# Modulation rows by TensorE alone, with unused products in its queue

## The chip, the cores and the metric

The kernel runs on one core of one Trainium2 chip. The metric is the device time of one execution in microseconds (us), as the median of several runs. Besides these, one execution was recorded by the hardware profiler; all views of the profile and of the trace are of that one.

The engines of the core are called as the profile calls them: PE is TensorE, the matrix engine (PEld is its loading of weights), DVE is VectorE, ACT is ScalarE, POOL is GpSimd, and SP is the queue from which most transfers are issued. Each works through its own instructions in the order in which they were written, and they meet through semaphores.

## The reference, cut to what matters

One sequence of 2048 tokens with 1024 channels goes through two modulated blocks: a Fourier mixing of tokens and channels, and an MLP with 3584 hidden units. Six rows of 1024 values that depend only on the vector `c` modulate them. Everything is float32.

```
mod = (_silu(c) @ w_mod).reshape(c.shape[0], 6, 1, -1)        # c: 1 x 1024, w_mod: 1024 x 6144
sa, ca, ga, sb, cb, gb = (mod[:, 0], mod[:, 1], ..., mod[:, 5])
h = _layernorm(x, axis=-1) * (1 + ca) + sa
x = x + ga * _A_ref(h, dft_seq_re, dft_seq_im, dft_hid_re, dft_hid_im)
h = _layernorm(x, axis=-1) * (1 + cb) + sb
x = x + gb * _B_ref(h, w1, b1, w2, b2)
```

`_A_ref` multiplies by the two DFT matrices of the channels and the two of the sequence and keeps the real part. `_B_ref` is a dense layer, a GELU and a second dense layer. The change concerns only the first two rows of `mod`, `sa` and `ca`: they are needed ahead of everything else, because the first matrix products read the normalized and modulated `h`.

## The kernel before, in words

**The opening.** `w_mod` is laid out as eight pieces of 128 rows of the inner dimension (k = 0 to 7). For `sa` and `ca` the kernel loads columns 0 to 2047 of each piece, 1 MB at a time, into `wm2(k)`. The SP queue is written out by hand: pieces 0 to 6, then the x tiles 0 and 8 (0.5 MB each), then piece 7, then the first tiles of the sequence DFT matrix (`in_cre_dram`, L692) and the other x tiles (L1424). Meanwhile ACT computes silu of `c` into `scol` and spreads it over 128 columns into `srep`, so that a product with `srep` gives the result on all 128 partitions at once.

The 2048 sums go into four banks of PSUM, 512 columns each: `mbank(0)` and `mbank(1)` hold `sa`, `mbank(2)` and `mbank(3)` hold `ca`. Two engines share the pieces:

- `mod_pe` takes k = 0, 3 and 5: four float32 products of 128 x 128 by 128 x 512 each (L474). For k = 0 the banks of `ca` are opened with a product of a single row of ones by ones (L473), which adds the 1 of `1 + ca`.
- `mod_dve` takes k = 1, 2, 4 and 6: DVE multiplies the piece by a column of `scol` and adds it up in `macc` (L479 for the first, L481 for the others). When that sum is done, four products with a matrix of ones (L1465) sum it over the partitions and add it to the banks.
- `mod_rows` takes k = 7 with four more products (L487) that close the four banks. Then DVE finds the largest absolute values of the banks (L507), from which a power of two is made as a scale (`m1`); ACT and DVE move the rows out of PSUM (L512, L518, L519) and finish x tile 0 in two halves (L494, L499, L517, L525, L504).

Between the two, DVE does the layer norm statistics of x tiles 0 and 8 (L592 to L617) and ACT begins the first tile of the DFT matrix (L681, with L684 on DVE).

**After the opening.** `plain1` multiplies tiles of `h` by tiles of the sequence DFT matrix: 16 steps of 48 float16 products (L1112). A float32 operand is split into a high and a low float16 part (ACT makes the high part, DVE the low part), and three products stand for one. Each step needs an x tile pair k, normalized by DVE and ACT (L633, L634, L635, L636), and a tile of the DFT matrix (L681, L684). The stages behind it (`winograd1`, L1162; the channel DFT, L1394; the two layers of the MLP, L1588 and L1697; transposes of the normalized tiles, L1296) are float16 products of the same size nearly throughout.

The order in which DVE, ACT and the transfers work from `plain1` on is set while the program is built: a planner keeps an estimated clock of each engine and picks the next task by due time. The opening isn't planned: it is written out by hand, and the planner's clocks are set by hand behind it (`clk.update(...)`). Neither these settings nor the planner's costs are touched by the change.

`ones` is a tile of 128 x 512 float32 ones that DVE writes at the start (L1432).

Of the kernel before, what the change touches and what calls it, by code (L numbers as in the profile page):

```python
# [9 lines left out]
F32 = mybir.dt.float32  # L10
F16 = mybir.dt.float16
I32 = mybir.dt.int32
AF = mybir.ActivationFunctionType
ALU = mybir.AluOpType
# [3 lines left out]
P = 128  # L18
# [17 lines left out]
def kernel(ctx, tc, x, cre, cim, dre, dim, w1, b1, w2, b2, c, wm, out):  # L36
# [13 lines left out]
    pe, act, dve, gp, sp = nc.tensor, nc.scalar, nc.vector, nc.gpsimd, nc.sync  # L50
# [8 lines left out]
    def mk(shape, dt, tag, bufs=1):  # L59
        cnt[0] += 1  # L60
        return pool.tile(shape, dt, tag=tag, name=f"{tag}_{cnt[0]}", bufs=bufs)
# [3 lines left out]
    def at(kb, n, dt=F32):  # L65

        w = n if dt == F32 else n // 2
        v = arena[:, int(kb * 256) : int(kb * 256) + w]
        return v if dt == F32 else v.bitcast(dt)
# [29 lines left out]
    O_H, O_SR, O_XF, O_OP, O_U, O_AUX = 0, 48, 80, 144, 168, 200  # L99
# [11 lines left out]
    def xf(i):  # L111

        k, n = i % 8, i // 8
        return at(O_Q[(0, 2, 1, 3)[k // 2]] + 8 * (k % 2) + 4 * n, 1024)
# [82 lines left out]
    def pow2(dst, src):  # L197

        dve.tensor_scalar(dst.bitcast(I32), src.bitcast(I32), 0x7F800000, None, op0=ALU.bitwise_and)
# [254 lines left out]
    scol, cc = mk([P, ND], F32, "scol"), mk([P, ND], F32, "cc")  # L454
    m1 = mk([P, 6], F32, "m1")
    srep = at(216, 1024).rearrange("p (k m) -> p k m", k=ND)
    mrow, ones = at(O_AUX, 1024), at(O_SO[0], 512)
    sas, ca1s = (at(o, 1024) for o in O_ROW)

    macc, mx = at(O_OP + 16, 2048), mk([P, 5], F32, "mx")  # L460

    def wm2(k):

        return at(O_U + 8 * k if k < 4 else O_H + 8 * (k - 4), 2048)

    def mbank(n):
        return banks8[:, 512 * n : 512 * n + 512]

    def mod_pe(k, first):

        for n in range(4):
            if first and n > 1:
                pe.matmul(mbank(n), ones[0:1, 0:P], ones[0:1, :], start=True, stop=False)  # L473
            pe.matmul(mbank(n), srep[:, k, :], wm2(k)[:, 512 * n : 512 * n + 512], start=first and n < 2, stop=False)  # L474

    def mod_dve(k, first):

        if first:
            dve.tensor_scalar(macc, wm2(k), scol[:, k : k + 1], None, op0=ALU.mult)  # L479
        else:  # L480
            dve.scalar_tensor_tensor(macc, wm2(k), scol[:, k : k + 1], macc, op0=ALU.mult, op1=ALU.add)  # L481

    def mod_rows(k, c_lo, x1):


        for n in (2, 3, 0, 1):
            pe.matmul(mbank(n), srep[:, k, :], wm2(k)[:, 512 * n : 512 * n + 512], start=False, stop=True)  # L487
        m, pm, sh, iu = (m1[:, j : j + 1] for j in range(4))
        (mv, cl), x_ = xs[0], xf(0)
        r, a = cl[:, 1, :], cl[:, 2, :]  # L490
        sl = [slice(512 * q, 512 * q + 512) for q in range(2)]

        def times_ca(q):
            dve.scalar_tensor_tensor(  # L494
                x_[:, sl[q]], x_[:, sl[q]], mv[:, 0, 0:1], mbank(2 + q), op0=ALU.subtract, op1=ALU.mult
            )

        def plus_sa(q):
            dve.scalar_tensor_tensor(  # L499
                x_[:, sl[q]], x_[:, sl[q]], r[:, 0:1], sas[:, sl[q]], op0=ALU.mult, op1=ALU.add  # L500
            )

        def lo(q):
            dve.tensor_tensor(hq[:, 3 * q, 0, 1], x_[:, sl[q]], hq[:, 3 * q, 0, 0], op=ALU.subtract)  # L504

        for j in (2, 3, 0, 1):
            dve.tensor_reduce(mx[:, j : j + 1], mbank(j), axis=AX.X, op=ALU.max, apply_absolute_value=True)  # L507
        dve.tensor_reduce(m, mx, axis=AX.X, op=ALU.max)
        pow2(pm, m)
        dve.reciprocal(sh, pm)  # L510
        dve.tensor_scalar(sh, sh, SH, None, op0=ALU.mult)
        act.activation(sas[:, sl[0]], mbank(0), AF.Copy, scale=sh)  # L512
        times_ca(0)
        dve.scalar_tensor_tensor(r, r, sh, a, op0=ALU.mult, op1=ALU.mult)
        plus_sa(0)
        x1.pop(0).run()
        act.activation(hq[:, 0, 0, 0], x_[:, sl[0]], AF.Copy)  # L517
        act.activation(sas[:, sl[1]], mbank(1), AF.Copy, scale=sh)  # L518
        act.activation(ca1s, banks8[:, 1024:2048], AF.Copy)  # L519
        x1.pop(0).run()  # L520
        c_lo.run()
        lo(0)
        times_ca(1)
        plus_sa(1)
        act.activation(hq[:, 3, 0, 0], x_[:, sl[1]], AF.Copy)  # L525
        x1.pop(0).run()
        lo(1)
        dve.tensor_scalar(iu, pm, 2.0**5 / SD, None, op0=ALU.mult)
# [169 lines left out]
    def opn(tb, m, kp):  # L698
        return 16 + 28 * (tb - 1) + 4 * CI[m] + kp
# [742 lines left out]
    act.activation(scol[:, :], cc[:, :], AF.Silu)  # L1442
    act.activation(warm[:, :], warm[:, :], AF.Sqrt)
    act.activation(srep, scol[:, :, None].to_broadcast([P, ND, P]), AF.Copy)
    for k in range(7):
        if k in (1, 2, 4, 6):
            mod_dve(k, k == 1)
        else:
            mod_pe(k, k == 0)
    for k in range(8):  # L1450
        if k in (0, 2, 3):
            c0[k][0].run()
# [8 lines left out]
    x0 = x_tasks(0)  # L1461
    for _ in range(12):
        x0.pop(0).run()
    for n in (2, 3, 0, 1):
        pe.matmul(mbank(n), ones[:, 0:P], macc[:, 512 * n : 512 * n + 512], start=False, stop=False)  # L1465
    c_hi, c_lo = c0[0][1]
    c_hi.run()
    x1 = x_tasks(1)
    for _ in range(2):
        x1.pop(0).run()  # L1470
    mod_rows(7, c_lo, x1)
    clk.update(act=34.0, dve=35.0, pe=34.0)
    done["mod"] = 33.0
# [11 lines left out]
    for tb in range(1, NTB):  # L1485
        for q in (0, 2, 1, 3) if tb == 1 else (1, 0, 2, 3):
            push("craw", "craw", [craw_load(tb, q, kp) for kp in range(4)], 0.0)
        for m in ORDER:
            for kp in range(4):
                n = opn(tb, m, kp)  # L1490
# [493 lines left out]
```

## Time and profile before

| | us |
|---|---|
| median of 3 runs | 1985.09 |
| lowest, highest | 1984.1, 1985.36 |
| profiled execution: its own time | 1985.24 |
| profiled execution: span from first to last instruction | 1983.5 |
| busy in the span: PE, DVE, ACT, POOL | 1954.0, 1426.3, 851.0, 192.0 |
| first product on PE starts | 7.11 |
| first product of `plain1` (L1112) starts | 38.48 |

A row of the timeline gives start and duration in us, the engine, the line of the kernel, the operation, the tiles that it writes and reads, shape and type, and how many instructions were merged into the row; in brackets stands the idle time of the engine ahead of the row and what ended it. One float32 product of 512 columns on PE is recorded as two instructions. Matmuls are pipelined, so the durations of neighbours overlap and the distance of two starts is the better measure. `arena` is the one large tile in which nearly everything lies, so most operands bear that name; the line tells them apart.

### The profile page before, as it was taken

What the parts mean: (1) busy time and instruction counts of PE and PEld (TensorE: products, weight loads), DVE (VectorE), ACT (ScalarE), POOL (GpSimd) and SP (SyncE); (2) the same over time, 40 slices, a digit from 0 to 9 for tenths busy, and PEclk for the clock granted to TensorE, in tenths of its full rate; (3) what the DMA queues carried; (4) which work ended last, traced back from release to release, by engine and by line L of the source; (5) the groups of instructions that cost most, each with busy time, mean ns of one, the idle gap of its engine ahead of it and who ended that gap; (6) DMA issues with size and microseconds to landing.
All of it is one profiled execution on the core that took longest, in us unless ns stands there. A gap on an engine that the chain in (4) does not pass through costs nothing. (4 is left out here: it accounts for less than half of the span.)

```text
span 1983.5 us, 23588 instructions
## 1 busy us (share of the span) xinstructions
PE 1954.0 (99%) x9004; PEld 888.6 (45%) x9004; DVE 1426.3 (72%) x1799; ACT 851.0 (43%) x1091; POOL 192.0 (10%) x282
## 2 busy tenths in 40 slices
PE   7999999999999999999999999999999999999999
PEld 2444444444444444444444444444444444444443
DVE  5977886898984477776688889999873453553566
ACT  3843331445542255554567466456223312312311
POOL 0012211221210012211010000000000000000000
PEclk9999999999999999999999999999999999999999
DMA  9148587688678867878674455454476432432324
GB/s 385 61 143 286 178 295 288 243 317 316 242 269 335 307 238 254 284 237 304 243 255 162 173 180 175 143 170 159 172 226 207 123 99 77 128 102 69 112 75 85
DMA packets 139362, 402.41 MB, mean 203 GB/s; under 512 B 15536, under 2 KB 15536, under 8 KB 134640
## 3 DMA queue, kind: packets, MB, share of 16 engines
q1 hardware_dynamic: 112528, 309.92, 45.9%
q0 software_dynamic: 26720, 90.98, 12.9%
q8 instruction: 70, 1.15, 0.2%
q14 instruction: 44, 0.36, 0.1%
HBM read 262.95 MB, written 137.89 MB: 202 GB/s over the span
## 5 line engine op out<-in xcount | busy, mean ns | idle before, releaser
L1697 PE MATMUL ps<-arena 128*128 128x512 f16 x2352 | 512.6, 380 | 4.1 <-DVE arena L1743 2.3
L1588 PE MATMUL ps<-arena 128*128 128x512 f16 x2352 | 510.2, 379 | 2.2 <-ACT arena L1610 2.2
L1162 PE MATMUL ps<-arena 128*128 128x512 f16 x2016 | 435.5, 379 | 1.5 <-DMA arena<-s 1.5
L1697 PEld LDWEIGHTS <-arena 128*128 128x128 f16 x2352 | 230.3, 98 | 283.9 <-issue 6.9
L1588 PEld LDWEIGHTS <-arena 128*128 128x128 f16 x2352 | 230.2, 98 | 279.4 <-issue 2.5
L1743 DVE SCALAR_TENSOR_TENSOR arena<-ps,i4c,arena 128x1024 f32<-128x1024 f32 x179 | 229.4, 1282 | 145.1 <-PE ps L1697 143.7
L1162 PEld LDWEIGHTS <-arena 128*128 128x128 f16 x2016 | 197.1, 98 | 239.6 <-DMA arena<-s 2.3
L1394 PE MATMUL ps<-arena 128*128 128x512 f16 x1344 | 292.4, 379 | 1.0 <-DMA arena<-u 1.0
L386 ACT ACTIVATE arena<-arena,shc 128x512 f16<-128x512 f32 (+1 forms) x115 | 115.9, 1018 | 278.9 <-PE ps L1697 186.3
L1394 PEld LDWEIGHTS <-arena 128*128 128x128 f16 x1344 | 131.4, 98 | 157.1 <-DMA arena<-u 1.5
L1112 PE MATMUL ps<-arena 128*128 128x512 f16 x768 | 168.8, 381 | 9.5 <-ACT arena L517 3.9
L411 DVE TENSOR_TENSOR arena<-arena 128x512 f32<-128x512 f32 (+1 forms) x228 | 171.1, 753 | 4.1
L681 ACT ACTIVATE arena<-arena 128x1024 f16<-128x1024 f32 x100 | 104.1, 1050 | 149.1 <-PE ps L1162 113.9
L398 DVE SCALAR_TENSOR_TENSOR arena<-arena,shc 128x512 f16<-128x512 f32 (+1 forms) x115 | 128.7, 1122 | 38.5 <-ACT arena L386 38.3
L684 DVE SCALAR_TENSOR_TENSOR arena<-arena 128x1024 f16<-128x1024 f32 x100 | 128.7, 1304 | 18.8 <-ACT arena L681 18.8
L1614 DVE TENSOR_TENSOR arena<-arena,ps 128x512 f32<-128x512 f32 x84 | 57.6, 686 | 111.1 <-PE ps L1588 107.0
L1607 ACT ACTIVATE arena<-arena,b1s,i1c 128x512 f32<-128x512 f32 x84 | 68.3, 813 | 137.0 <-DVE arena L1614 137.0
L1112 PEld LDWEIGHTS <-arena 128*128 128x128 f16 x768 | 75.0, 98 | 103.6 <-issue 5.4
L773 ACT ACTIVATE arena<-arena 128x1024 f16<-128x1024 f32 x56 | 57.8, 1048 | 62.7 <-DMA u<-arena 21.8
L776 DVE TENSOR_TENSOR arena<-arena 128x1024 f16<-128x1024 f32 x56 | 66.9, 1218 | 14.7 <-ACT arena L773 14.7
L386 ACT ACTIVATE arena<-arena,s1c 128x512 f16<-128x512 f32 (+1 forms) x70 | 60.8, 883 | 35.8 <-DVE arena L411 24.9
L398 DVE SCALAR_TENSOR_TENSOR arena<-arena,s1c 128x512 f16<-128x512 f32 (+1 forms) x70 | 66.3, 959 | 11.2 <-ACT arena L386 11.0
(161 smaller groups left out, 1400.5 us busy)
## 6 DMA issues: line engine op xcount, KB each, us to landing
w<-arena SPq DMA_DIRECT2D x64, 512.0 KB, 5.1
arena<-w SPq DMA_DIRECT2D x119, 256.0 KB, 2.7
u<-arena POOLq DMA_DIRECT2D x56, 512.0 KB, 5.0
arena<-u SPq DMA_DIRECT2D x112, 256.0 KB, 4.1
arena<-w SPq DMA_DIRECT2D x56, 512.0 KB, 3.6
arena<-s SPq DMA_DIRECT2D x48, 512.0 KB, 7.6
arena<-in_cre_dram SPq DMA_DIRECT2D x32, 512.0 KB, 6.7
arena<-in_cim_dram SPq DMA_DIRECT2D x32, 512.0 KB, 5.6
```

The lines of the kernel that those rows point to most:

```text
L386: act.activation(o[m][0], q(j), AF.Copy, **sc)
L398: dve.scalar_tensor_tensor(o[m][1], q(j), scale, o[m][0], op0=ALU.mult, op1=ALU.subtract)
L411: dve.tensor_tensor(q(d), q(a), q(b), op=op)
L681: h = Task("act", 1.15, lambda: act.activation(o[:, :, 0], s2, AF.Copy, scale=SC), list(deps) + free)
L684: dve.scalar_tensor_tensor(o[:, :, 1], s2, SC, o[:, :, 0], op0=ALU.mult, op1=ALU.subtract)
L1112: pe.matmul(bank_of(d_), hleft(d_, s, kp, a), cop(n)[:, s, b], start=(kp == 0 and s == 0 and a == 0 and b == 0), stop=(kp == 7 and s == 1 ...
L1162: pe.matmul(bank_of(st + ch), left, cop(n)[:, s, b], start=(start and kp == 0 and s == 0 and a == 0 and b == 0), stop=(kp == 3 and s == 1 ...
L1394: pe.matmul(bank_of(bk), up(N)[:, c_, a], dp(n)[:, c_, w], start=(start and ri == 0 and c_ == 0 and i == 0), stop=(ri == 1 and c_ == 3 and ...
L1588: pe.matmul(ps.rearrange("p (k t) -> p k t", k=4), w1c[:, m, s, a, d * P : (d + 1) * P], zc(m)[:, b, :, d, :], start=(start and d == 0 and ...
L1607: act.activation(dst, src, AF.Gelu_apprx_tanh, scale=inv, bias=b1s[:, 2 * p + j : 2 * p + j + 1])
L1697: pe.matmul(t[:, j], hidc[:, c_, m, a, k * P : (k + 1) * P], w2c[:, m, c_, w], start=(start and c_ == 0 and n == 0), stop=(c_ == 1 and n = ...
L1743: lambda: dve.scalar_tensor_tensor(dst, ps[b], inv, dst, op0=ALU.mult, op1=ALU.add), kp[b],
```

## The change

All of the pieces 0 to 6 go to `mod_pe`; `mod_dve`, `macc` and the four products that closed the sum of DVE are taken out. A new function `idle_pe(n)` puts n products of the constant `ones`, read as float16, into PE's queue. They write bank 5, which nothing reads before `plain1` opens it anew. Sixteen of them stand ahead of piece 0, three behind each of the pieces 0 to 6, and seventeen behind piece 7. Transfers, their order, and the other instructions of DVE, ACT and POOL stay.

```
-    macc, mx = at(O_OP + 16, 2048), mk([P, 5], F32, "mx")
+    mx = mk([P, 5], F32, "mx")
...
-    def mod_dve(k, first):
-
-        if first:
-            dve.tensor_scalar(macc, wm2(k), scol[:, k : k + 1], None, op0=ALU.mult)
-        else:
-            dve.scalar_tensor_tensor(macc, wm2(k), scol[:, k : k + 1], macc, op0=ALU.mult, op1=ALU.add)
+    def idle_pe(n):
+
+        w = ones.bitcast(F16)
+        for _ in range(n):
+            pe.matmul(mbank(5), w[:, 0:P], w[:, 0:512], start=True, stop=True)
...
     def mod_rows(k, c_lo, x1):
         for n in (2, 3, 0, 1):
             pe.matmul(mbank(n), srep[:, k, :], wm2(k)[:, 512 * n : 512 * n + 512], start=False, stop=True)
+        idle_pe(17)
...
     act.activation(srep, scol[:, :, None].to_broadcast([P, ND, P]), AF.Copy)
+    idle_pe(16)
     for k in range(7):
-        if k in (1, 2, 4, 6):
-            mod_dve(k, k == 1)
-        else:
-            mod_pe(k, k == 0)
+        mod_pe(k, k == 0)
+        idle_pe(3)
...
-    for n in (2, 3, 0, 1):
-        pe.matmul(mbank(n), ones[:, 0:P], macc[:, 512 * n : 512 * n + 512], start=False, stop=False)
```

## The prediction

> **What bounds the kernel now.** I read the page first: the span is TensorE's (PE).
>
> ```profile
> span 1983.5 us, 23588 instructions
> PE 1954.0 (99%) x9004; PEld 888.6 (45%) x9004; DVE 1426.3 (72%) x1799; ACT 851.0 (43%) x1091; POOL 192.0 (10%) x282
> ...
> PEclk9999999999999999999999999999999999999999
> ```
>
> The profiled execution took 1985.24 us, 1.74 us of it outside the span; the median of the three runs, 1985.09, is 0.15 lower. The change touches only the opening, so I read the timeline of the first 60 us, PE first. Its columns are start, duration, engine, line, operation and count; brackets hold the idle time ahead and what ended it. A float32 product of 512 columns shows as two records.
>
> ```profile
> 7.11 3.75 PE L474 MATMUL ps<-arena 128*128 128x512 f32 x4 [7.11 <-DMA arena<-in_wm_dram]
> 10.79 2.07 PE L473 MATMUL ps<-arena 1*128 1x512 f32 x2
> 12.79 2.08 PE L474 MATMUL ps<-arena 128*128 128x512 f32 x2
> 14.80 2.07 PE L473 MATMUL ps<-arena 1*128 1x512 f32 x2
> 16.80 10.95 PE L474 MATMUL ps<-arena 128*128 128x512 f32 x18
> 27.59 3.60 PE L1465 MATMUL ps<-arena 128*128 128x512 f32 x8
> 31.02 3.60 PE L487 MATMUL ps<-arena 128*128 128x512 f32 x8
> 38.48 0.39 PE L1112 MATMUL ps<-arena 128*128 128x512 f16 x1 [3.86 <-ACT arena L517]
> ...
> 47.90 4.92 PE L1112 MATMUL ps<-arena 128*128 128x512 f16 x22 [0.66 <-DVE arena L636]
> 54.31 0.38 PE L1112 MATMUL ps<-arena 128*128 128x512 f16 x1 [1.49 <-ACT arena L681]
> 55.76 4.48 PE L1112 MATMUL ps<-arena 128*128 128x512 f16 x20 [1.07 <-DVE arena L684]
> ```
>
> From 7.11 to 34.6 PE has no gap: it is behind its data. The pitch (start to start) tells the clock. At L1465 eight records pass between 27.59 and 31.02, 0.429 us each; at 7.11 four pass until 10.79, 0.92 each. Two narrower stretches of the same view place the change of pace.
>
> ```profile
> 17.82 5.22 PE L474 MATMUL ps<-arena 128*128 128x512 f32 x6
> ...
> 22.08 5.67 PE L474 MATMUL ps<-arena 128*128 128x512 f32 x12
> ```
>
> From 17.82 to 22.08 five records pass, 0.85 each; the twelve from 22.08 end at 27.59, 0.46 each. So PE ran at half speed until about 22.5, through 15 us of unbroken work; the page's clock row, full in every slice, doesn't show it. Now VectorE (DVE) and, last row, ScalarE (ACT):
>
> ```profile
> 0.94 0.48 DVE L1432 MEMSET arena<- 128x512 f32 x1
> ...
> 9.54 1.29 DVE L479 TENSOR_SCALAR arena<-arena,scol 128x2048 f32<-128x2048 f32 x1 [8.10 <-DMA arena<-in_wm_dram]
> 12.02 2.35 DVE L481 SCALAR_TENSOR_TENSOR arena<-arena,scol 128x2048 f32<-128x2048 f32 x1 [1.19 <-DMA arena<-in_wm_dram]
> 16.98 2.35 DVE L481 SCALAR_TENSOR_TENSOR arena<-arena,scol 128x2048 f32<-128x2048 f32 x1 [2.61 <-DMA arena<-in_wm_dram]
> 22.08 2.35 DVE L481 SCALAR_TENSOR_TENSOR arena<-arena,scol 128x2048 f32<-128x2048 f32 x1 [2.74 <-DMA arena<-in_wm_dram]
> ...
> 32.08 0.69 DVE L507 TENSOR_REDUCE mx<-ps 128x1 f32<-128x512 f32 x1 [3.59 <-PE ps L487]
> ...
> 28.43 1.06 ACT L681 ACTIVATE arena<-arena 128x1024 f16<-128x1024 f32 x1 [0.73 <-DMA arena<-in_cre_dram]
> ```
>
> The four DVE steps start as pieces 1, 2, 4 and 6 of w_mod land: one piece in 2.5 us. Then come two x tiles, of one piece's bytes together, and piece 7, so an estimate for that is 22.08 + 2 x 2.5 = 27.1; the cre tile, next in the queue, was there by 28.43. DVE's four steps (1.29 + 3 x 2.35 = 8.34 us) lie between waits for data, and DVE then waits 3.59 us for PE's last step, L487. PE sets when the modulation rows are ready.
>
> What follows belongs to DVE, not PE. One stretch of the windows (length, busy time and count of PE, PEld, DVE, ACT, POOL), and two rows of who waited for whom in it:
>
> ```profile
> 36.00:121.00 85.00, 76.92 (x343) 33.51 (x344) 78.70 (x118) 59.16 (x89) 1.27 (x1) 0.98 0.34 120
> ...
> DVE arena L636 <- ACT arena L635: 3.5, 8, 0.8
> ...
> ACT arena L635 <- DVE arena L634: 22.7, 13, 3.9
> ```
>
> DVE is busy 78.7 of 85 us making the normalized tiles, and its longest wait in sum is for ACT, which waits for DVE far more. PE finds its last tile late twice, then runs through:
>
> ```profile
> 119.31 0.60 PE L1112 MATMUL ps<-arena 128*128 128x512 f16 x2 [0.80 <-ACT arena L635]
> 120.58 92.33 PE L1112 MATMUL ps<-arena 128*128 128x512 f16 x427 [0.67 <-DVE arena L636]
> 212.75 212.54 PE L1162 MATMUL ps<-arena 128*128 128x512 f16 x984
> 426.76 23.48 PE L1162 MATMUL ps<-arena 128*128 128x512 f16 x108 [1.47 <-DMA arena<-s]
> ```
>
> So the path is: PE's modulation products, then DVE's chain to 120.58, then PE to the end. A shift of the first is handed to the end.
>
> **The change part by part.** PE's modulation stretch lasts from 7.11 to 31.02 + 3.43 = 34.45 now. Each edit against that:
>
> The closing products of the DVE sum (L1465) go: 8 records x 0.429 = -3.43.
>
> Pieces 1, 2, 4 and 6 come to PE: 4 x 8 x 0.429 = +13.73. PE takes 3.43 us for a piece that lands every 2.5, so this lies wholly on the path; the data hides none of it.
>
> Three unused float16 products behind each of seven pieces: at the 0.216 of the row at 120.58 (92.33 / 427), 21 x 0.216 = +4.53. They wait for nothing and nothing overtakes them; since the next piece has landed already, they are pure delay. For the hand-over between float16 and float32 the nearest rows are the transposes:
>
> ```profile
> 725.49 5.34 PE L1394 MATMUL ps<-arena 128*128 128x512 f16 x24
> 730.67 1.04 PE L1296 MATMUL ps<-ident,arena 128*128 128x128 f32 x8
> ```
>
> 24 x 0.216 = 5.18 is just the distance of the two starts: no hand-over, and I take 0.
>
> The sixteen unused products ahead of piece 0 need only the constant, ready at 1.42. At half speed (0.427, twice 0.216) they last until 1.5 + 6.8 = 8.3, at full speed until 5.0. If the clock rises on the way, they end between 6.6 and 8.3; piece 0 then starts 0 to 1.2 late. I take +0.3.
>
> With the clock up, piece 0 and its two one-row products (12 records) cost 12 x 0.429 = 5.15. Now they last from 7.11 to about 18.66 (the last two of them lead the 18 records at 16.80), 11.55: -6.40. Of this 11.55, 12 x 0.852 = 10.2 is pace and 1.3 comes at the changes between L473 and L474. At full pace these cost between 0 and 1.3; I take half, +0.6, since the rest halves too. Piece 3, until 27.59 - 3.43 = 24.16, costs 5.50 now and 3.43 then: -2.07.
>
> Sum: -3.43 + 13.73 + 4.53 + 0.3 - 6.40 + 0.6 - 2.07 = +7.3, bounds +6.4 and +8.9: PE's last row product ends at about 41.7.
>
> The four DVE steps that go save nothing: they lay in idle time, and DVE's next work waits for x and then for PE. The seventeen unused products behind the rows cost 17 x 0.216 = 3.67 of the 38.48 - 34.45 = 4.03 that PE waits there: hidden. What they buy is clock:
>
> ```profile
> 36.20:39.60 3.40, 0.77 (x2) 1.00 1.03 406
> 39.60:43.03 3.43, 2.87 (x7) 0.54 1.03 411
> ```
>
> After a stretch with 0.77 us of work the next 3.43 us were granted half speed, some 1.7 us of PE's work. It pays nothing: PE later waits at 47.90, 54.31, 55.76 and 119.31 for DVE and ACT, whose chain doesn't wait for PE there. Were that cover gone, it would be -1.7. No DMA moves in its queue, and no order of DVE or ACT changes.
>
> So the end moves by +7.3: 1985.24 + 7.3 = 1992.5 against the profiled execution, 1992.4 against the median.
>
> **Rivals.** *The clock rises late or falls back.* Now it stayed at half speed through 15 us, in which the one-row products (L473) ran from 10.79 to 12.79 and 14.80 to 16.80; it rose in the first 3.4 us without them. If they count as idleness, piece 0 can close it again after the warm-up; if it simply takes 15 us from PE's start, it rises near 17. The first costs one stretch at half speed, +1.7, or all of piece 0, 11.55 - 5.75 = +5.8. In the second PE starts piece 0 at 8.3, 0.9 later than I took, and does half of its work in the 8.6 us until 17: 0.9 + 4.3 = +5.2. Together 1994.1 to 1998.2. Against it: the gap that dropped the clock at 39.6 held 0.77 us of work, while in piece 0 full-height products fill about half of any such stretch. The Trainium skill ("TensorE: Matmul & The Clock Gate", Part 1) says that about 3.4 us of sustained work open the gate and an idle window of that length closes it. By that rule the old kernel would have been at full speed by 14, not 22.5; here the trace disagrees with it. Taken literally it gives the new kernel my sum, and no price to piece 0.
>
> *Bound by arrival, faster.* Dropping the DVE detour wins if PE keeps pace with the data. Then the end is piece 7's landing at 27.1 plus its own products. It decides if a piece and three unused products fit 2.5 us, at a pitch of (2.5 - 0.65) / 8 = 0.23. Then PE ends at 27.1 + 1.9 = 29.0, 5.5 earlier: 1979.6. No float32 row of 512 columns shows a pitch under 0.43.
>
> *Absorbed later.* PE waits 1.47 at 426.76. If the store behind it doesn't move, this wait hides 1.5, and other late waits as much more; half of 7.3 gone gives about 1988.7. Against it: those transfers hang on buffers that DVE and PE free, which move too.
>
> *It doesn't do what it says.* If the three products per piece bridged real gaps, they would be free, -4.5: 1987.9. PE has no gap there now and gets more work.
>
> **How the numbers follow.** Forecast 0.80, late clock 0.09, absorbed 0.05, bridging 0.03, arrival 0.03. The likeliest case gives 1992.4; its bounds give 1991.5 to 1994.0, and the three runs spread 1.3. The range reaches down towards the absorbed case and up into the late clock: 1989.8 to 1995.4. About 0.2% (4 us) is what a measurement here can tell from no change: faster 0.03; same 0.06, the absorbed and bridging cases for the most part; slower 0.91.
>
> **What would show it.** Right: the first L474 record near 7.1 to 8.3, pitch 0.43 from it on; no PE gap up to the last L487, which ends near 41.7; DVE's first L507 about 7.3 later than 32.08, and the row of PE that began at 120.58 moved by the same; no half clock behind the tile wait. Wrong: PE gaps between the pieces, a pitch near 0.85 behind the warm-up, or a start of the long run at 120.58 that moved less than L487.

## The result, and the profile after

The changed kernel takes 1992.23 us, the median of six runs (1989.94 to 1993.56); the kernel before took 1984.59 in its six (1978.83 to 1985.37). The ratio is 1.0047, with a 95% interval of 1.0036 to 1.0058: slower, and more than the 0.2% that a measurement here can tell from no change. The two medians alone give 1.0038, inside that interval; in microseconds the interval stands for +7.1 to +11.5. The forecast was 1992.4, or +7.3.

Two lines of the page after, span and busy times. PE has 15 us more work, DVE 9 us less, and the span is 6.9 us longer:

```profile
span 1990.4 us, 23735 instructions
...
PE 1969.1 (99%) x9082; PEld 896.5 (45%) x9082; DVE 1417.3 (71%) x1795; ACT 851.1 (43%) x1091; POOL 190.5 (10%) x282
```

The timeline of PE in the opening, changed kernel. L480 is the unused products, L486 the last step of the rows (L487 before):

```profile
1.48 5.47 PE L480 MATMUL ps<-arena 128*128 128x512 f16 x16 [1.48 <-DVE arena L1432]
7.13 1.96 PE L474 MATMUL ps<-arena 128*128 128x512 f32 x4 [0.17 <-DMA arena<-in_wm_dram]
9.01 1.12 PE L473 MATMUL ps<-arena 1*128 1x512 f32 x2
10.06 1.13 PE L474 MATMUL ps<-arena 128*128 128x512 f32 x2
11.12 1.15 PE L473 MATMUL ps<-arena 1*128 1x512 f32 x2
12.20 2.08 PE L474 MATMUL ps<-arena 128*128 128x512 f32 x2
14.07 1.49 PE L480 MATMUL ps<-arena 128*128 128x512 f16 x3
15.35 3.67 PE L474 MATMUL ps<-arena 128*128 128x512 f32 x8
18.86 0.81 PE L480 MATMUL ps<-arena 128*128 128x512 f16 x3
...
39.91 3.60 PE L486 MATMUL ps<-arena 128*128 128x512 f32 x8
43.34 3.83 PE L480 MATMUL ps<-arena 128*128 128x512 f16 x17
47.42 0.39 PE L1112 MATMUL ps<-arena 128*128 128x512 f16 x1 [0.24 <-ACT arena L517]
```

No row behind that of 7.13 and ahead of 47 has an idle time in brackets: PE is behind its data throughout. Its last step starts 8.89 us later (39.91 for 31.02), the first product of the main stage 8.94 (47.42 for 38.48). DVE has given its share away and waits for PE instead; two rows of its timeline:

```profile
23.21 1.29 DVE L592 BATCH_NORM_STATS2 xst<-arena 128x6 f32<-128x512 f32 x2 [21.77 <-DMA arena<-in_x_dram]
...
40.97 0.69 DVE L507 TENSOR_REDUCE mx<-ps 128x1 f32<-128x512 f32 x1 [13.60 <-PE ps L486]
```

The wait for PE at L507 has grown from 3.59 to 13.60 us. The rows from 12.20 to 15.35 are slow (two records and three unused products take 3.15 us); the windows show why. Columns: stretch, length, PE busy and count, granted clock, DMA share, GB/s:

```profile
8.50:11.50 3.00, 3.00 (x7) 1.00 1.01 426
11.50:15.30 3.80, 3.80 (x7) 0.58 1.00 425
```

PE was busy without a gap and still was granted half speed for about one stretch of 3.4 us (the second row averages over a little more than that). The shift is then handed on, and partly given back far behind:

```profile
129.51 92.33 PE L1112 MATMUL ps<-arena 128*128 128x512 f16 x427 [0.67 <-DVE arena L636]
221.68 18.51 PE L1162 MATMUL ps<-arena 128*128 128x512 f16 x85
...
958.38 2.76 PE L1394 MATMUL ps<-arena 128*128 128x512 f16 x12 [1.92 <-DMA arena<-u]
...
1119.53 10.52 PE L1694 MATMUL ps<-arena 128*128 128x512 f16 x48 [1.24 <-DVE arena L1740]
1130.30 2.75 PE L1694 MATMUL ps<-arena 128*128 128x512 f16 x12 [0.24 <-DVE arena L1740]
```

At 129.51 (120.58 before) and at 221.68 (212.75 before) the shift is 8.93. At the end it is 6.9. The same late place in the kernel before, one row of its timeline and one of its windows:

```profile
1111.25 14.80 PE L1697 MATMUL ps<-arena 128*128 128x512 f16 x60 [2.30 <-DVE arena L1743]
...
1112.00:1115.00 3.00, 3.00 (x8) 0.50 0.00 0
```

There PE waited 2.30 us once and then lost 1.7 to a stretch at half speed; after the change it waits 1.24 and 0.24 and the clock stays up, 2.5 better. Two other waits bring it to about 2.0: the one at 958.38 is 0.94 longer than its fellow at 948.62, and one near 1044 is 0.42 shorter.

### The profile page after: what moved, and what is told of

Its sections match the earlier page's. It is cut to its first block, busy times and chain, and to the rows that moved or that the text cites. A ratio compares the mean times of both kernels' runs of the same rounds, so it can differ in the third digit from the quotient of the medians.

```text
span 1990.4 us, 23735 instructions
## 1 busy us (share of the span) xinstructions
PE 1969.1 (99%) x9082; PEld 896.5 (45%) x9082; DVE 1417.3 (71%) x1795; ACT 851.1 (43%) x1091; POOL 190.5 (10%) x282
## 5 line engine op out<-in xcount | busy, mean ns | idle before, releaser
L1162 PE MATMUL ps<-arena 128*128 128x512 f16 x2016 | 435.5, 379 | 1.4 <-DMA arena<-s 1.4
L1162 PEld LDWEIGHTS <-arena 128*128 128x128 f16 x2016 | 197.1, 98 | 239.5 <-DMA arena<-s 1.9
```

The source lines that it names most:

```text
L1162: pe.matmul(bank_of(st + ch), left, cop(n)[:, s, b], start=(start and kp == 0 and s == 0 and a == 0 and b == 0), stop=(kp == 3 and s == 1 ...
```

## The experiments

Theory: PE's queue up to the last step of the rows is the path, and its end is handed to the end of the kernel; the clock counts how much of the array works, so products of one row count as idleness. Each experiment changes one part of this; the cuts of code show the decisive lines alone, and `idle_pe` is defined as in the change. Rivals: the unused products are needed to hold the clock; the clock rises or falls for another cause; the chain behind the rows has slack.

**The changed kernel without the three unused products per piece.**

```
         mod_pe(k, k == 0)
-        idle_pe(3)
```

> The changed kernel without the 21 unused products between the pieces. Theory (PE's queue is the path, they are pure delay): the last step of the rows starts 21 x 0.216 = 4.5 earlier than the 39.91 of the changed kernel, at about 35.4, and the time falls by as much, to about 1987.7. Rival (they hold the clock up): without them the clock falls for at least one more stretch of 3.4 us, each worth 1.7 us, so the last step starts at 37 or later and the time stays above 1989.

1987.58 us; ratio to the kernel before, which ran beside it, 1.0029 (1.0017 to 1.0041), where the full change had 1.0047. Its timeline:

```profile
11.92 23.42 PE L474 MATMUL ps<-arena 128*128 128x512 f32 x50
35.18 3.60 PE L486 MATMUL ps<-arena 128*128 128x512 f32 x8
...
216.97 23.26 PE L1162 MATMUL ps<-arena 128*128 128x512 f16 x107
```

The last step starts 4.73 earlier than with them, the next stage 4.71 earlier: they were pure delay (21 x 0.216 = 4.5, and 0.25 is an earlier start of piece 0). The 50 records from 11.92 take 0.465 each, against 0.429 at full speed; 50 x 0.036 = 1.8 is again just one stretch at half speed, no more than with the unused products. They hold nothing up, and the rival is out.

**The changed kernel with full-height products for the one-row ones.**

```
-   pe.matmul(mbank(n), ones[0:1, 0:P], ones[0:1, :], start=True, stop=False)
+   pe.matmul(mbank(n), ones[:, 0:P], part, start=True, stop=False)   # part: 1/128
```

`part` is a tile of 128 x 512 that DVE fills with 1/128 at the start.

> The changed kernel with the two one-row products of piece 0 replaced by products over all 128 rows (ones by 1/128, the same sum). Theory (the clock counts how much of the array works, and one-row products count as idleness): the stretch at half speed from about 12 to 15.4 us disappears, piece 0 lasts 5.2 us and not 6.9, the last step of the rows starts at about 38.2, and the time falls by 1.7 to about 1990.5. Rival (the clock falls for another cause, such as the float32 form or the change between forms): the half-speed stretch stays and so does the start at 39.9.

1990.82 us; ratio 1.0043 (1.0028 to 1.0058), which doesn't differ from the full change's. The trace does (lines are two higher in this kernel):

```profile
6.84 1.95 PE L476 MATMUL ps<-arena 128*128 128x512 f32 x4 [0.32 <-DMA arena<-in_wm_dram]
...
12.07 0.81 PE L482 MATMUL ps<-arena 128*128 128x512 f16 x3
...
37.20 3.60 PE L488 MATMUL ps<-arena 128*128 128x512 f32 x8
...
9.00:12.00 3.00, 3.00 (x8) 1.00 1.01 429
12.00:16.00 4.00, 4.00 (x12) 1.00 1.02 426
```

Piece 0 takes 5.23 us and not 6.94, the clock stays at 1.00 (last two rows, windows), and the last step starts 2.71 earlier. That is 0.29 for the earlier start, 1.7 for the stretch at half speed, and some 0.76 for the four changes between one row and all rows, 0.19 each (9.01 to 10.06 is 1.05 where two records at full height take 0.86). The forecast of 38.2 had only the 1.7. With one-row products the clock falls although PE is busy with them, and with full-height ones it doesn't. The short gaps at the changes go with them too; the kernel before with full-height products, below, speaks to those.

**The kernel before with the sixteen leading products alone.**

```
     act.activation(srep, scol[:, :, None].to_broadcast([P, ND, P]), AF.Copy)
+    idle_pe(16)
```

> The kernel before with one part of the change alone: the sixteen unused products ahead of piece 0. Theory (PE's half-speed start is on the path, and the share that DVE takes keeps PE ahead of the data): PE waits for pieces 3 and 5 and for DVE's sum, which is ready at 24.4; its four closing products and the four of piece 7 follow, so the last step starts at about 28 and not 31.0, and the time falls by about 3, to about 1982. If the one-row products close the clock in between, the waits for data hide it. Rival (DVE's chain from there to 120 us has slack, or the warm clock isn't on the path): within 1 us of the kernel before.

1982.78 us, with the kernel before at 1981.85 beside it; ratio 1.0001 (0.999 to 1.0012). But the trace has what the theory asked for:

```profile
24.41 3.70 PE L1472 MATMUL ps<-arena 128*128 128x512 f32 x8 [1.25 <-DVE arena L481]
27.95 3.60 PE L493 MATMUL ps<-arena 128*128 128x512 f32 x8
...
209.69 93.40 PE L1168 MATMUL ps<-arena 128*128 128x512 f16 x432
```

PE now waits for DVE's sum, its last step starts at 27.95, and the next stage starts 3.06 earlier than in the first profile of the kernel before (212.75). The forecast was right against that profile and wrong against the median, where the rival's "within 1 us" came true. One way out is that the kernel before itself opens so in some executions: its 26 times of this comparison spread from 1976.78 to 1987.91.

**The kernel before with the seventeen products behind the rows alone.**

```
             pe.matmul(mbank(n), srep[:, k, :], wm2(k)[...], start=False, stop=True)
+        idle_pe(17)
```

> The kernel before with the seventeen unused products behind the rows alone. Theory (the first tile's products wait for DVE and ACT, not for PE): the clock stays at full speed between 36 and 47 us, the start of the long run of PE at 120.6 stays within 0.3, and the time is within 1 us of the kernel before. Rival (PE's half-speed stretch from 39.6 to 43.0 is on the path): 1.7 us faster.

1981.53 us; ratio 1.0001 (0.9991 to 1.001).

```profile
30.43 3.60 PE L493 MATMUL ps<-arena 128*128 128x512 f32 x8
33.86 3.83 PE L487 MATMUL ps<-arena 128*128 128x512 f16 x17
...
40.00:44.00 4.00, 3.85 (x18) 1.00 1.03 410
...
212.15 28.22 PE L1169 MATMUL ps<-arena 128*128 128x512 f16 x130
```

From 40 to 44, where the first profile of the kernel before shows half speed, the clock is full. From the last step to the next stage it is 181.72 us with them and 181.73 without: the clock that they buy is worth nothing, as PE waits for DVE there. All starts lie some 0.6 earlier than in the first profile (the next stage 0.60), where at most 0.3 was expected: piece 0 started 0.50 earlier in this execution (6.61 for 7.11), which has nothing to do with products behind the rows.

**The kernel before, profiled twice more**, unchanged, for what the third experiment left open.

> The kernel before once more, unchanged, for a second profiled execution: 26 further times of it spread from 1976.8 to 1987.9. Theory (the moment at which its clock rises depends on how the clock's 3.4 us stretches happen to lie against the one-row products): an execution near 1981 has its clock up by about 10 to 14, and its last step L487 starts near 28, not 31.0; one near 1985 rises late, as the first profile did. Rival (the opening is always the same, the spread arises later): L487 starts at 31.0 whatever the time, and the difference appears behind 120 us.

> The same once more, as a third profiled execution. Theory and rival as for the second: the start of L487 (28 to 31) and of PE's long run (117.5 to 120.6) go with the time, or the start stays at 31.0.

The two took 1980.88 and 1983.74 us. The first one's timeline, with two rows of its windows at the end:

```profile
10.74 1.31 PE L473 MATMUL ps<-arena 1*128 1x512 f32 x2
11.97 1.12 PE L474 MATMUL ps<-arena 128*128 128x512 f32 x2
...
24.39 3.70 PE L1465 MATMUL ps<-arena 128*128 128x512 f32 x8 [0.62 <-DVE arena L481]
27.92 3.60 PE L487 MATMUL ps<-arena 128*128 128x512 f32 x8
...
10.90:14.30 3.40, 3.40 (x7) 1.00 1.00 424
14.30:17.70 3.40, 3.40 (x5) 0.54 1.01 422
```

and the second one's:

```profile
14.82 2.07 PE L473 MATMUL ps<-arena 1*128 1x512 f32 x2
...
31.04 3.60 PE L487 MATMUL ps<-arena 128*128 128x512 f32 x8
```

So the opening has two forms. In one the clock rises near 11, when the first one-row product has just begun; these products then close it for one stretch (0.54), and L487 starts at 27.92. In the other it stays at half speed past them, and L487 starts at 31.04, as in the first profile. 3.1 us lie between them, and the next stage starts 3.13 apart (table below). So the first profile, on which the forecast rests, is one of two forms. These are three executions; how often each form occurs was not counted.

**The kernel before with full-height products for the one-row ones** (the edit of the second experiment on the kernel before).

> The kernel before with the two one-row products of piece 0 replaced by products over all 128 rows (ones by 1/128, the same sum); no unused products. Theory (one-row products count as idleness): the clock is up one or two stretches of 3.4 us after PE's start, by 14 at the latest, L487 starts at about 28, and the profiled execution is 3 faster than the first profile of the kernel before, about 1982. Rival (the clock needs 15 us of any work): it rises near 22 and L487 starts at about 31.

1981.26 us; ratio 0.9988 (0.998 to 0.9997).

```profile
10.62 1.91 PE L475 MATMUL ps<-arena 128*128 128x512 f32 x2
12.32 1.12 PE L476 MATMUL ps<-arena 128*128 128x512 f32 x2
...
24.37 3.70 PE L1468 MATMUL ps<-arena 128*128 128x512 f32 x8 [1.25 <-DVE arena L483]
27.91 3.60 PE L489 MATMUL ps<-arena 128*128 128x512 f32 x8
...
12.60:36.40 23.80, 17.59 (x40) 1.00 1.02 410
36.40:39.81 3.41, 2.77 (x7) 0.50 1.03 407
```

The last two rows are of its windows. Two records take 1.91 us at 10.62 and 1.12 at 12.32: the clock rises near 12 and isn't closed again, and L489 starts at 27.91. As the kernel before can rise early too (its second profile), this alone would prove little. But the half-speed stretch behind the tile wait tells how the stretches lie; in the first profile of the kernel before it is this one:

```profile
39.86:43.27 3.41, 3.11 (x8) 0.50 1.03 410
```

39.86 and 36.40 are 3.46 us apart, one stretch of 3.41 but for 0.05, so the stretches of the two executions lie alike. Counted back from there (an estimate), both had one from about 9.1 to 12.5. With full-height products it ended with the clock up; with one-row products in it from 10.79 on it didn't. Fifteen us of any work are not needed. Nor do short gaps explain it: PE waits 1.25 us for DVE ahead of 24.37 here and keeps its clock from 12.60 to 36.40, and the gaps at the four changes are 0.76 us in all.

In the times this version lies 0.12% under the kernel before. The interval leaves 1 out, but that is less than the 0.2% that a measurement here can tell from no change. The profiled execution took 1982.99, 2.25 less than the first profile where 3 was expected; the opening gave 3.1, and 0.9 was lost in the stages behind.

**The changed kernel without its sixteen leading products.**

> The changed kernel without its sixteen unused products ahead of piece 0. Theory (PE's queue is the path, so half speed at its start counts in full): the clock rises 3.4 to 13 us after 7.1, each 3.4 us at half speed costs 1.7, less the 1.7 that the stretch at half speed cost anyway; the last step of the rows starts between 40 and 45 instead of 39.9, and the time is 1993 to 1997. Rival (the lead buys nothing, as the pieces come slowly anyway): the start stays within 0.5 of 39.9 and the time at 1992.

1994.12 us (1992.07 to 2003.31); ratio 1.0059 (1.0042 to 1.0076), whose interval overlaps that of the full change.

```profile
10.33 1.12 PE L473 MATMUL ps<-arena 1*128 1x512 f32 x2
...
41.23 3.60 PE L486 MATMUL ps<-arena 128*128 128x512 f32 x8
...
222.99 17.21 PE L1162 MATMUL ps<-arena 128*128 128x512 f16 x79
```

In this execution the clock rose near 10 (two records at 10.33 take 1.12 us), some 3.4 us after the first product, and the last step still starts 1.32 later than with the lead. So the lead is on the path here; in the times it isn't separated from the noise. Two further runs took 1999.75 and 2003.31. A clock that rises late may be part of it, but they were not profiled, so their cause is open.

All ten profiled executions together: start of the rows' last step, start of the stage behind the first one (L1162 before), and what is left from there to the end of the span:

| | last step | next stage | between | left |
|---|---|---|---|---|
| before, first profile | 31.02 | 212.75 | 181.73 | 1770.7 |
| before, second and third | 27.92, 31.04 | 209.62, 212.75 | 181.70, 181.71 | 1769.5, 1769.2 |
| changed | 39.91 | 221.68 | 181.77 | 1768.8 |
| without the threes | 35.18 | 216.97 | 181.79 | 1767.0 |
| changed, full height | 37.20 | 218.98 | 181.78 | 1770.3 |
| changed, without the lead | 41.23 | 222.99 | 181.76 | 1770.0 |
| before, lead alone | 27.95 | 209.69 | 181.74 | 1770.7 |
| before, tail alone | 30.43 | 212.15 | 181.72 | 1771.7 |
| before, full height | 27.91 | 209.62 | 181.71 | 1771.6 |

The third column spans 0.09 us while the first spans 13.3: the opening is handed on whole. The last column spans 4.7 us and doesn't follow the opening. Part of it is the clock: in six of the ten executions it fell for one stretch between the next stage and the last products, and these six have 1770.6 left on average, the other four (the third of the kernel before, the changed one, that without the threes, that with the lead alone) 1768.9, which is 1.7 less.

## Why the prediction was right

The path was as forecast: PE's queue, then DVE's chain, then PE to the end. That the number came out within 0.2 us is luck: the opening cost 1.6 more than the sum, and the stages behind it gave back 2.0 that no term had. The last step of the rows ended at 43.34 and not at 41.7, and behind the warm-up one stretch ran at the half-speed pitch that the prediction had named as a sign of being wrong. The terms one by one:

- **Pieces given to PE, unused products between them.** Right. From 15.35 to 39.91 six pieces and six fills take 24.56 us; the terms gave 6 x (3.43 + 0.65) = 24.5. Taking the fills out returned 4.7.
- **Start of piece 0.** Taken +0.3, measured 0.02 (7.13 for 7.11).
- **Changes between one-row and full-height products.** Taken 0.6, measured 0.19 x 4 = 0.76.
- **The clock.** Mis-sized: the main sum had it up throughout. It fell for one stretch, +1.7, which is the first form of the late-clock rival at its lower price. With it, 7.3 - 0.3 + 0.16 + 1.7 makes 8.86, and the opening shows 8.89. The argument against that rival, that full-height products fill about half of any stretch, didn't hold; at full pace the two one-row products and their changes fill 2.1 us (9.01 to 10.06 and 11.12 to 12.20), which is more than half of a stretch of 3.4.
- **Tail of seventeen, and DVE's four steps.** Both worth nothing, as forecast; the first shown by itself, the second by the wait of 13.60.
- **Handing on to the end.** Whole until 221.68, then 2.0 less. The absorbed rival doesn't explain it: a wait for the store is still there (1.36 at 316.44, for 1.47 at 426.76 before). The first profile of the kernel before had a clock stretch and a longer wait near 1111 that the changed one hadn't. That is not the change's doing: the third profile of the kernel before opens like the first and has no such stretch, and against it the changed one is some 8.5 longer: 8.9 in the opening, and 0.4 less behind it (table).
- **The base.** The forecast rested on a profile with the late clock. Against executions with the early one the same opening costs 12.0 us (39.91 for 27.92). The ratio of the times, 1.0047 or some 9.3 us, lies between 8.9 and 12.0, as it would if both forms occur among the runs; but the medians alone give 7.6, and the share of the forms isn't known.

On the rule from the Trainium skill ("TensorE: Matmul & The Clock Gate", Part 1), that about 3.4 us of sustained work open the gate: the kernel before with full-height products agrees (up near 12 after a start at 7.08, ahead of the 14 that the prediction worked out from it), the first profile (22.5) doesn't, because of the one-row products.

## What to carry to other kernels

An engine that is behind its data has no wait to fill: work put there to hold the clock is paid in full (4.5 us for 21 products here), and the pitch of the records tells it before anything is built. Where the clock matters, look at what the products fill, not at whether PE is busy: two one-row products in a queue cost a stretch at half speed, or kept the clock down for 15 us. Only one row and all 128 were tried; what lies between isn't shown. And profile the kernel before more than once when its times spread: the one that was recorded may not be the usual one.

## What the runs showed that was not expected

A busy PE can lose its clock: 1.00 to 0.58 in the stretch from 11.50, with no gap, behind one-row float32 products; full-height ones in their place kept it at 1.00. The same program opens in two forms 3.1 us apart, by when its clock rises. And the same wait costs differently from one execution to the next: the first layer of the MLP begins behind a wait of 2.20 or 2.21 us in all ten profiles (996.77 in the first of the kernel before, 1006.54 in the changed one). In seven, these two among them, the 60 products behind it take 13.11 us; in the other three they take 14.80, 1.7 more, with the clock at half speed for one stretch. How the wait lies to the stretches may decide it; that isn't shown.
